# An attention and feed-forward kernel: two PSUM slots become two tensors, nine early masks move to one pair of banks, and the order of work is listed anew

## The chip, the cores and the metric

One Trainium2 chip, one core. The kernel is one launch. The metric is device time in microseconds; the kernel before has a median of 805.13 us over 3 runs (803.35 to 806.81). Lower is better. A program of some 17,900 instructions runs on five engines: TensorE (PE, with its weight loads as PEld), VectorE (DVE), ScalarE (ACT), GpSimd (POOL), and SyncE (SP), which issues DMAs.

## The reference: top-32 attention, then a gated feed-forward layer

```python
# attention: q, k, v are (4, 8, 576, 64)
scores = scale * np.matmul(q, k.transpose(0, 1, 3, 2))
kth = np.partition(scores, -32, axis=-1)[..., -32:-31]
scores = np.where(scores >= kth, scores, -1e9)
attn = softmax(scores);  out = attn @ v
# feed-forward on x, (2304, 512): 4 * 576 tokens, 8 heads * 64
h = x @ w_in                      # w_in is (512, 2048)
g = h * np.tanh(log1p(exp(h)))
return g @ w_out                  # w_out is (2048, 512)
```

All of it is wanted in float32 accuracy. The weights arrive as 64-bit floats.

## The kernel before, in words

**Attention.** The work is cut into 80 units. A unit is one tile of 128 query rows for a pair of heads (for the last 64 rows both heads share one tile). Each head's part of a unit is a slot, a 128 x 576 matrix of scores; there are 144 slots, numbered in order, and several tables (`CB`, `MB`, `PBO`, `PBH`) choose by slot number how a step is done. A unit goes: scores by matmul into the ring psW (line 701), eviction to S by ScalarE (720), eight-at-a-time maxima on VectorE for a threshold guess (736 to 750), a count of what lies below the guess (765 on ScalarE or 769 on VectorE), a multiply that leaves only the values of interest (773), a small rank compare on 9 elements (776), and one more maximum (779) that gives the exact threshold. Then come the mask and the exponential, a reciprocal (850), the division (875 and 877), transposes (900), evictions (906), the product with V (938) and a copy into xr (959 and 979), which holds the tokens for the feed-forward layer.

**The mask** of a slot is done in one of three ways. The usual one takes the exponential of the scores on ScalarE (843) and multiplies it by the comparison with the threshold on VectorE (845). For slots in `MB` ScalarE forms a large penalty (835), GpSimd subtracts it (837) and ScalarE takes the exponential (839). For slots in `PBO` and `PBH` ScalarE forms a relu of threshold minus score in the buffer EM (814; one buffer), TensorE adds score and penalty in PSUM (823, 824), and ScalarE takes the exponential straight from PSUM (827). This third way needs two PSUM banks: those of the output accumulators (psO) for `PBO`, those of the up-projection (psH) for `PBH`. A slot in `PBO` or `PBH` is done by matmul even where `MB` holds it too.

**Feed-forward.** Tokens go in 9 groups of 256. A group's tokens are split in a high and a low part (xh and xl; 1034, 1039 and 1045). The up-projection `m1` (1068) computes hidden blocks of 128 in pairs, 72 pairs in all: each half of a pair is 12 matmuls of 128 x 256 into one half of a slot of 512 columns. A pair is evicted from PSUM to mb by ScalarE (1074) or VectorE (1076), then goes through tanh, arctan and sin on ScalarE (1080, 1099, 1100; in batches, since these need other tables than the exponential), a multiply (1115), a cast to GH (1120 and 1122), a subtraction to GL (1130), and the down-projection (1149 for the first group, 1153 for the others) into psO. Line 1211 or 1213 evicts psO.

**PSUM.** It has eight banks of 512 float32 columns. psW is a ring of four tensors of one bank. The up-projection has two slots, which are two halves of one tensor psHH of 1024 columns; after the last unit two of psW's tensors are lent to it as slots 3 and 4. psO is likewise one tensor psOO of 1024 columns, used as two halves.

**What sets the order.** Each step is an entry of a plan (`P.op`) with an engine, a duration, what it depends on, and what buffer slots it takes and frees. Some entries have several ways, that is, engines that can do them. The list `ORDER` holds, for the main program, the number of each of the 4,931 entries and the way chosen. The plan walks through that list, gives each entry a start time from the durations, sorts by it, and issues the instructions in that sequence; every engine runs its own in order. The waits between engines are then derived from the tensors that the issued instructions read and write. Two things follow the plan's times beside the sequence: filler matmuls on TensorE in long planned gaps, and an extra wait of a GpSimd step for a VectorE step that has just been planned (lines 1285 to 1289).

Of the kernel before, what the change touches and what calls it, by code (L numbers as in the profile page):

```python
# [49 lines left out]
PBO = (2, 8, 12, 16)  # L50
PBH = (0, 2, 6, 10, 20, 28, 31, 138)
# [40 lines left out]
    b"AHT#qu83Xz_T6@Js;k@C!cyX=l%&0k^z%PfFQ%;>Y-A(kI$e~1TNSE#y_}iFxLV8i{Qc9bvR%QEOI6L*&0f*n4(q7o?C{Ff$=yZ$?~EIkn+J#2"
    b"B+PoR@N^>TkXGt?XnApAd~h1eeO73Dkku*N-aPmnni__S7BAOYrMJ_UNYE#dR~anv)HVvF`9}NQ*cV2j(&!A`m3}N=fz|A#I%|0O^!)V=*ZLb9"
    b"EaqQiv?MS{(8PGDuvox)Q<K$x0qa)#2ZgT>4hUXj#@rwtA`vRI!F-d*TG3_eY}RZH3yImhcGJO7$?$bj(iU3+t=7wIJg_-vi>>S-IZFlk*x+4}"
    b"hpms;$16H*4Y6}}h<mer?~dI{%AwnK9>i@_+2^?2C1RInLSk5?>L%AcH#bLlZE)Lvt28M&H6`6WZH33t=-U}F$F}Sa-xGCWYuTaGZ@mvBa8;C_"
    b"tlV~|s<!&nzW47|o*9hY8|SlYM}0(QL)Omyhga3yJAQV1&XK0Xx^s8WHxAwZ5Sf&_yE%G~URvJ83(3PN2M$JEiO)EZy6!=G_T&7A1+7<O4t;Dn"
    b"y7$wu&zByxJ^3<v`D7e7{u!A-yjJ*>ay)MTncTyq&Qm-c^se^qOy+YcJFBQdzxeBTNvwh4k(cp3wCgWM#u$7o0p4%?XM0~63Fe6}TD&B%@B8}x"
    b"bHcZSE=U9?{8)Ov?DU~a1EL~7O)rW~Od03@s+N^BdA)4fBHL{8&Tl#S#6L+^<~CB6Gk>ofp50(=Z!7IAbopwEql2AGh->IIOlq=X{E<qfG=+_B"
    b"VNUx$6yy|@7ABO)6sI3o-gG@&B`NV%otlPMO__(f=H?qK>aj6ZH}960Cs(AXZaHyVD>c1B`}WqfqZ!BVRJ(6mUa1pNbF9|0%6p~m_7j;WPi16g"
    b"-C5-~>|5!xb5~7$-Q%MtA6!57>9c=TR>0}((;sWABUd-no~duByLTq%?wSYtqVDdv(75~F+19nWjrW`Ln$BH#*toZC|DNXT^Iw{tJUpB8=xNKn"  # L100
    b"`<Jg=jLv@?Q*fZY?PBY*k(Q^U2a7Kqh`oC7(37v%#)?Wh#yh)<;|gCKe);X~sr%=iz0PkxpBsDq`H}AvJzX8_mw7iz;uDe*Q*IR8?ELZbS7~=z"
    b"a%x7;rGZ=N$9hX&bzQyL@aApr(aFB!ulrwB^i7|<e(QJH?RW1_l|MK!_59Dwjls$@Ls`|Cq^g>~vvqgwo~wPwg)74jV#wSK3hn*b#`@C@=Re+K"
    b"Qgd?YLwKIN4^6`tK4o7V$^U$<pymFh2VX{;#|XTvX1<4)uROZh^zG|+;yC;2HG#qwK_UJ}KPMjk5S|o?w%J{3^{DV_(dAoL9{>8&I@2aTJ@xm="
    b"(<0H|V(rg5W+f#skNI1Rd9j@(-L?+g(o$WrIJ~?}x0Ah{W7{(xIcEiz=UnPa&tL56aVIQy^>TYs{^Dg+FLCdyeaid$qBUNsC<^p@d-!;+h*3ST"
    b"a+Q{*_QBX5-wrih9X~#jVBf$YLt!%bab6U6B;oMW!Z$DaJKJA%^}Z6J>oNRAlj7GVt`1B|*6%-_X0Uk4x&U!zkpyeKQAzPqq11s8<Ljm-p*Pl)"
    b"n%%No_WI4Ijlt>WCvJvGR+Me1JXv0S>UKs@=FzH}w|$$$2HxEXuibpCuKujlxzk(DSiJuH#`10dyRGkItglC$-<~z};KTduyE$JzZ2KsEV29P`"
    b"!I6fciQ(LPjR#|QHd)6Vmf4ke@lfQ2eA@z9yGxfHoxVQ&bmU9(_{g{Wqw!-&2`!1=l2cNDJ{p(*{(5-uyWEeTkK62jO@5qJQoY7C@heTe^~t2o"
    b"Q-v!(rqbIpj*cq+cD-@SZRXkE<9{eB8q{N@<sDNuJG-W5Pcu$*zp21HfA>P!z3k*|%~RDcx!#_^_Vha7@Z3CVm6<hlRp5Kjn05Ai?I3}c^Io6+"
    b"fLNc`kb7Y$`(ji6LxZo=T4TCei?m5(9W0(zfV;#);QnxL_>m#|K9l(I(`UWQByua|>XmD}g^x$tzBG>(E#@nJ)<S#ol)r<~-swy={@SIjTS6aW"
    b"F?reid^#@Q3<dS{4LrJ^8wI@RSt9hZ_tom9YemJDPY5nrEMPMJeSeJEsvp9hUOz>bEHx4`T_$d9VkTy4F1$>{(xR__#kw`#<`RLylB?GT1<Pz0"  # L110
    b"nEEAYA+>UHT3S}_z;F43e-soCS%<8#@{x+2QHrziQ&Cp^Ya43sV0XkZ-o<~Wq<<a8S1lmaN!=~U)qQiy^|c-wo!1K-7Qb<GLqb@ZM(L*TjOB^9"
# [1232 lines left out]
```

## Time and profile before

| | |
|---|---|
| median of 3 runs | 805.13 us (803.35 to 806.81) |
| profiled execution | 804.39 us, span 802.5 us |
| TensorE busy | 761.6 us (95%), weight loads 597.3 us |
| VectorE, ScalarE, GpSimd busy | 679.3, 658.6 and 518.8 us |
| mean granted TensorE clock | 0.992 of full speed |

The span runs from the first to the last instruction; the execution is 1.9 us longer. Busy time of an engine is the union of its instructions. An engine's idle time is put down to whatever released the instruction after it. Matmuls are pipelined, so one that is shown with 0.28 us is followed by the next after some 0.12.

### The profile page before, as it was taken

What the parts mean: (1) busy time and instruction counts of PE and PEld (TensorE: products, weight loads), DVE (VectorE), ACT (ScalarE), POOL (GpSimd) and SP (SyncE); (2) the same over time, 40 slices, a digit from 0 to 9 for tenths busy, and PEclk for the clock granted to TensorE, in tenths of its full rate; (3) what the DMA queues carried; (4) which work ended last, traced back from release to release, by engine and by line L of the source; (5) the groups of instructions that cost most, each with busy time, mean ns of one, the idle gap of its engine ahead of it and who ended that gap; (6) DMA issues with size and microseconds to landing.
All of it is one profiled execution on the core that took longest, in us unless ns stands there. A gap on an engine that the chain in (4) does not pass through costs nothing.

```text
span 802.5 us, 17921 instructions
## 1 busy us (share of the span) xinstructions
PE 761.6 (95%) x5697; PEld 597.3 (74%) x5697; DVE 679.3 (85%) x3067; ACT 658.6 (82%) x1372; POOL 518.8 (65%) x765
## 2 busy tenths in 40 slices
PE   8789999988999999999999999999999999999995
PEld 5556677755768878768878777787878787889983
DVE  6999999999999889999999998999899989813531
ACT  5999999999899889798999787889898689457540
POOL 3888897888676666778678576765666666313130
PEclk9999999999999999999999999999999999999998
DMA  5424456643324322330222322323242122203343
GB/s 159 149 80 148 127 155 227 234 169 132 129 87 141 90 89 60 101 113 25 84 82 60 127 86 84 93 82 96 67 125 67 59 83 79 83 15 89 89 116 92
DMA packets 56792, 83.70 MB, mean 104 GB/s; under 512 B 5872, under 2 KB 28656, under 8 KB 56688
## 3 DMA queue, kind: packets, MB, share of 16 engines
q1 hardware_dynamic: 56464, 82.19, 33.1%
q8 instruction: 47, 0.77, 0.4%
q14 instruction: 57, 0.47, 0.2%
q10 hardware_dynamic: 224, 0.28, 0.1%
HBM read 66.72 MB, written 8.13 MB: 93 GB/s over the span
## 4 chain that ended last, share of the span: by engine, by line
PE 61%; ACT 14%; DVE 9%; POOL 7%; issue 3%; DMA 3%; SPq 0%; ACTq 0%; POOLq 0%; DVEq 0%
PE psO L1153 19%; PE psH L1068 19%; PE psW L701 7%; PE psW L938 7%; PE psW L900 5%; POOL Y L773 3%; DVE Y L845 2%; ACT S L720 2%; ACT tb L1100 2%; DVE C L736 1%; ACT Y L843 1%; PE psW L1068 1%; DVE M L779 1%; PE psO L1149 1%; ACT WT L906 1%
## 5 line engine op out<-in xcount | busy, mean ns | idle before, releaser
L773 POOL TENSOR_TENSOR Y<-Y,S 128x576 f32<-128x576 f32 x126 | 178.4, 1422 | 27.4 <-DVE Y L845 8.2
L736 DVE MAX8 C<-S 128x8 f32<-128x82 f32 (+1 forms) x1008 | 170.8, 230 | 8.7 <-ACT S L720 7.9
L1068 PE MATMUL psH<-xh,wih 128*128 128x256 f32 x544 | 163.1, 300 | 4.8 <-ACT mb L1074 3.1
L1068 PE MATMUL psH<-xl,wih 128*128 128x256 f32 x544 | 153.6, 282 | 0.0
L1068 PE MATMUL psH<-xh,wil 128*128 128x256 f32 x544 | 153.4, 282 | 0.0
L701 PE MATMUL psW<-KS,QS 64*128 64x288 f32 (+1 forms) x576 | 121.1, 459 | 4.6 <-DMA QS<-in_q_dram 2.1
L720 ACT COPY S<-psW 128x288 f32<-128x288 f32 x288 | 108.9, 406 | 18.5 <-PE psW L701 18.0
L779 DVE MAX8 M<-Y 128x8 f32<-128x585 f32 x144 | 109.0, 760 | 7.8 <-POOL Y L773 5.5
L1068 PEld LDWEIGHTS psH<-xh,wih 128*128 128x128 f32 x544 | 103.7, 191 | 15.5 <-ACT mb L1074 5.8
L1153 PE MATMUL psO<-woh,GH 128*128 128x512 f32 x256 | 107.7, 421 | 0.0
L845 DVE SCALAR_TENSOR_TENSOR Y<-S,M,Y 128x576 f32<-128x576 f32 x120 | 99.4, 841 | 7.2 <-ACT Y L843 6.8
L1068 PEld LDWEIGHTS psH<-xl,wih 128*128 128x128 f32 x544 | 103.7, 191 | 1.5 <-issue 0.2
L1068 PEld LDWEIGHTS psH<-xh,wil 128*128 128x128 f32 x544 | 103.5, 190 | 0.0
L843 ACT ACTIVATE Y<-S,SM 128x576 f32<-128x576 f32 x120 | 93.4, 785 | 11.6 <-DVE M L779 10.9
L1130 POOL TENSOR_TENSOR GL<-mb,GH 128x256 fp32r<-128x256 f32 x93 | 69.4, 750 | 46.2 <-DVE GH L1120 22.5
L900 PE MATMUL psW<-ident,Y 128*128 128x128 f32 (+1 forms) x640 | 82.3, 270 | 10.9 <-ACT Y L877 3.0
L938 PEld LDWEIGHTS psW<-WT,V 128*64 128x64 f32 x1280 | 64.2, 138 | 33.6 <-ACT WX L924 14.8
L900 PEld LDWEIGHTS psW<-ident,Y 128*128 128x128 f32 (+1 forms) x640 | 62.9, 140 | 34.8 <-ACT Y L877 7.2
L938 PE MATMUL psW<-WT,V 128*64 128x128 f32 (+1 forms) x1280 | 81.9, 271 | 6.8 <-ACT WX L924 6.3
L906 ACT COPY WT<-psW 128x512 f32<-128x512 f32 (+1 forms) x142 | 74.5, 553 | 15.5 <-PE psW L900 15.2
L746 DVE MAX8 M<-C 128x8 f32<-128x56 f32 x432 | 83.4, 208 | 1.8
L769 DVE TENSOR_SCALAR_CACHE_REDUCE Y<-S,M 128x576 f32<-128x576 f32 x98 | 78.5, 804 | 7.1 <-PE psW L917 5.5
(167 smaller groups left out, 1720.2 us busy)
## 6 DMA issues: line engine op xcount, KB each, us to landing
WL<-wld SPq DMA_DIRECT2D x104, 256.0 KB, 2.7
V<-in_v_dram SPq DMA_DIRECT2D x28, 320.0 KB, 3.1
mb<-in_moe_w_in_dram SPq DMA_DIRECT2D x16, 512.0 KB, 3.8
mb<-in_moe_w_out_dram SPq DMA_DIRECT2D x16, 512.0 KB, 4.2
KS<-in_k_dram SPq DMA_DIRECT2D x27, 288.0 KB, 3.2
QS<-in_q_dram SPq DMA_DIRECT2D x80, 64.0 KB, 2.7
woh<-mb SPq DMA_DIRECT2D x16, 256.0 KB, 2.9
wld<-woh SPq DMA_DIRECT2D x13, 256.0 KB, 2.5
```

The lines of the kernel that those rows point to most:

```text
L701: nc.tensor.matmul(psW[P.slot[wks[n]]][:, 0:HS], g_("QS", qs)[hp, :], KSt()[hp, rng], start=True, stop=True)
L720: return lambda: eng(St(n)[:, rng], psW[P.slot[w]][:, 0:HS])
L736: nc.vector.max(Ct(n)[:, j, :], St(n)[:, EDGE[j]:EDGE[j + 1]])
L746: cur[n] = P.op("dve", dve(8 * NCH), lambda n=n, r=r: nc.vector.max(M8()[:, n, r, :], Ct(n)), [cur[n]], free=[("C", ck[n])] if r == 2 else ...
L773: y = either(pool2(S), held(S), lambda eng, n=n: eng.tensor_tensor(Yt(n), Yt(n), St(n), op=ALU.mult), [c], prio=pr + 0.5 + OFF[5])
L779: ym.append(P.op("dve", dve(S + PAD), lambda n=n: nc.vector.max(M8()[:, n, 3, :], Yw(n)), [y, x], prio=pr + 0.6 + OFF[6]))
L843: e = P.op("act", acts(S, 1), lambda n=n: nc.scalar.activation(Yt(n), St(n), AF.Exp, scale=scale, bias=SM()[:, 0, n:n + 1]), [nm, ym[n]], ...
L845: mk.append(P.op("dve", held(S, 68), lambda n=n: nc.vector.scalar_tensor_tensor(Yt(n), St(n), th(n), Yt(n), op0=ALU.is_ge, op1=ALU.mult, a ...
L900: nc.tensor.transpose(psW[P.slot[wk]][:, t_ * w:(t_ + 1) * w], Yt(n)[hp, c_:c_ + 128], ident[hp, hp])
L938: nc.tensor.matmul(psX[64 * h:64 * h + 64, 0:n_], lw, rhs, start=t_ == 0, stop=t_ == T)
L1068: nc.tensor.matmul(w, a, b_, start=n == 0, stop=n == len(mm) - 1)
L1153: nc.tensor.matmul(psO[t], c[:, ts_], y, start=f == 0 and n == 0, stop=f == NF - 1 and n == 2)
```

## The change

The two slots of the up-projection become two tensors of 512 columns. The table `PBH` goes. `PBO` becomes (0, 2, 6, 8, 9, 10, 12, 16, 20): slots 0, 6, 10 and 20 move from the up-projection's pair to the accumulators', slot 9 goes from the usual mask to the mask by matmul, slots 28 and 138 go from matmul to the usual mask, and slot 31, which `MB` holds, from matmul to GpSimd's mask. Slots 2, 8, 12 and 16 stay. Some planned durations of small steps change, and `ORDER` is another list.

```diff
-PBO = (2, 8, 12, 16)
-PBH = (0, 2, 6, 10, 20, 28, 31, 138)
+PBO = (0, 2, 6, 8, 9, 10, 12, 16, 20)
...
 ORDER = (
...
     psW = [ps.tile([128, 512], F32, name=f"psW{i}") for i in range(Z["W"])]
-    psHH = ps.tile([128, 1024], F32, name="psH")
     psOO = ps.tile([128, 1024], F32, name="psO")
-    psH = [psHH[:, 0:512], psHH[:, 512:1024]] + psW[0:2]
+    psH = [ps.tile([128, 512], F32, name=f"psH{i}") for i in range(2)] + psW[0:2]
     psO = [psOO[:, 0:512], psOO[:, 512:1024]]
...
-                nm = P.op("pool", 0.15, lambda: nc.gpsimd.tensor_scalar(
+                nm = P.op("pool", 0.19, lambda: nc.gpsimd.tensor_scalar(
...
-                        c = P.op("pool", 0.15, lambda n=n, c24=c24: nc.gpsimd.tensor_scalar(
+                        c = P.op("pool", 0.21, lambda n=n, c24=c24: nc.gpsimd.tensor_scalar(
...
-                    x = either(0.29, 0.129, lambda eng, n=n: eng.tensor_scalar(
+                    x = either(0.38, 0.125, lambda eng, n=n: eng.tensor_scalar(
...
-                lg = P.op("pool", 0.15, lambda: nc.gpsimd.tensor_scalar(
+                lg = P.op("pool", 0.19, lambda: nc.gpsimd.tensor_scalar(
...
-                by = "O" if n0 + n in PBO else "H" if n0 + n in PBH else None
+                by = "O" if n0 + n in PBO else None
...
-                    bk = [(by, key + ("pb", n, i)) for i in range(1 if by == "O" else 2)]
-                    pb = psOO if by == "O" else psHH
+                    bk = [(by, key + ("pb", n, i)) for i in range(1)]
+                    pb = psOO
...
-                    e = P.op("pool", pool2(S), lambda n=n: nc.gpsimd.tensor_tensor(
+                    e = P.op("pool", 1.18, lambda n=n: nc.gpsimd.tensor_tensor(
...
-            rzo = P.op("pool", 0.15, lambda: nc.gpsimd.tensor_scalar(
+            rzo = P.op("pool", 0.24, lambda: nc.gpsimd.tensor_scalar(
...
-            rzo = P.op("dve", 0.13, rz, [rzo, lg], free=[("M8", m8k)], prio=pr + 0.8 + OFF[6])
+            rzo = P.op("dve", 0.07, rz, [rzo, lg], free=[("M8", m8k)], prio=pr + 0.8 + OFF[6])
```

Both lists are compressed, so the diff does not show what they hold. Decoded, each has 4,931 entries. TensorE's part is nearly the same: in both, the first `m1` comes after 24 score steps, 18 transposes and 8 products with V, the 49th after 86, 80 and 40, and the 85th after 60 products with V. The engines chosen for steps with several ways differ as follows (before to after):

| step (line) | GpSimd | VectorE | ScalarE |
|---|---|---|---|
| multiply (773) | 126 to 121 | 18 to 23 | |
| rank compare (776) | 40 to 23 | 104 to 121 | |
| division (875, 877) | 31 to 35 | 5 to 6 | 72 to 67 |
| sum of a row (852, 854) | 38 to 31 | | 42 to 49 |
| high part of tokens (1034, 1045) | 10 to 16 | 5 to 3 | 21 to 17 |
| eviction of a pair (1074, 1076) | | 14 to 10 | 58 to 62 |
| product with the gate (1115) | 49 to 51 | 23 to 21 | |
| cast to GH (1120, 1122) | 22 to 23 | 13 to 6 | 29 to 35 |
| subtraction to GL (1130) | 95 to 90 | 33 to 38 | |

## Rows read from the trace of the kernel before

**Rows 1.** The page, busy time: us, share of the span, instructions.

```profile
PE 761.6 (95%) x5697; PEld 597.3 (74%) x5697; DVE 679.3 (85%) x3067; ACT 658.6 (82%) x1372; POOL 518.8 (65%) x765
```

**Rows 2.** Windows: length, then busy us of each engine with instructions; clock, DMA.

```profile
0.00:200.00 200.00, 178.25 (x1260) 123.39 (x1262) 183.83 (x870) 181.25 (x411) 159.87 (x256) 0.98 0.50 158
200.00:680.00 480.00, 471.90 (x3695) 376.73 (x3693) 446.54 (x2080) 417.94 (x866) 331.31 (x471) 1.00 0.29 88
680.00:802.50 122.50, 111.42 (x752) 97.22 (x748) 48.89 (x119) 59.38 (x97) 27.61 (x39) 0.98 0.28 79
```

**Rows 3.** Groups, whole span: busy us, mean ns, idle us before with releasers.

```profile
L1068 PE MATMUL psH<-xh,wih 128*128 128x256 f32 x544 | 163.1, 300 | 4.8 <-ACT mb L1074 3.1 <-DVE mb L1076 1.5
...
L1068 PEld LDWEIGHTS psH<-xh,wih 128*128 128x128 f32 x544 | 103.7, 191 | 15.5 <-ACT mb L1074 5.8 <-issue 5.0 <-DVE mb L1076 2.2
...
L1074 ACT COPY mb<-psH 128x512 f32<-128x512 f32 x56 | 32.9, 590 | 13.6 <-PE psH L1068 13.5
...
L1076 DVE COPY mb<-psH 128x512 f32<-128x512 f32 x10 | 6.9, 688 | 12.2 <-PE psH L1068 12.0
```

**Rows 4.** Groups of line 1068 from 200 to 680 us.

```profile
L1068 PE MATMUL psH<-xh,wih 128*128 128x256 f32 x372 | 111.8, 301 | 2.1 <-ACT mb L1074 1.6 <-DVE mb L1076 0.3
```

**Rows 5.** Groups of line 1068 from 680 us on.

```profile
L1068 PE MATMUL psH<-xh,wih 128*128 128x256 f32 x96 | 27.7, 289 | 1.6 <-DVE mb L1076 1.1 <-ACT mb L1074 0.5
```

**Rows 6.** Waits from 200 to 680 us: total us, times, longest us.

```profile
ACT mb L1074 <- PE psH L1068: 10.0, 9, 1.5
```

**Rows 7.** Timeline near 700 us: start, us, instruction, idle before.

```profile
699.95 0.28 PE L1068 MATMUL psH<-xh,wil 128*128 128x256 f32 x1
...
701.27 0.28 PE L1068 MATMUL psH<-xl,wih 128*128 128x256 f32 x1
...
701.39 0.28 PE L1068 MATMUL psH<-xh,wil 128*128 128x256 f32 x1
701.70 0.69 DVE L1076 COPY mb<-psH 128x512 f32<-128x512 f32 x1 [2.54 <-PE psH L1068]
...
702.45 0.39 PE L1068 MATMUL psH<-xh,wih 128*128 128x256 f32 x1 [0.78 <-DVE mb L1076]
```

**Rows 8.** Timeline near 645 us.

```profile
645.90 0.28 PE L1068 MATMUL psH<-xh,wil 128*128 128x256 f32 x1
...
646.22 0.59 ACT L1074 COPY mb<-psH 128x512 f32<-128x512 f32 x1 [1.40 <-PE psH L1068]
...
646.85 0.39 PE L1068 MATMUL psH<-xh,wih 128*128 128x256 f32 x1 [0.68 <-ACT mb L1074]
```

**Rows 9.** Timeline near 758 us, where psW is lent to the up-projection.

```profile
757.91 0.68 DVE L1076 COPY S<-psW 128x512 f32<-128x512 f32 x1
...
758.63 0.28 PE L1068 MATMUL psW<-xh,wil 128*128 128x256 f32 x1
```

**Rows 10.** Timeline near 675 us: the mask of slot 138, and what follows.

```profile
674.75 1.02 PE L823 MATMUL psH<-S,ident 128*128 128x512 f32 x2
...
676.09 0.48 PE L1153 MATMUL psO<-woh,GH 128*128 128x512 f32 x1
```

**Rows 11.** Groups, whole span, of the side work that moves.

```profile
L845 DVE SCALAR_TENSOR_TENSOR Y<-S,M,Y 128x576 f32<-128x576 f32 x120 | 99.4, 841 | 7.2 <-ACT Y L843 6.8
...
L776 DVE TENSOR_SCALAR Y<-ranks,SM 128x9 f32<-128x9 f32 x71 | 14.7, 210 | 0.0
...
L773 DVE TENSOR_TENSOR Y<-Y,S 128x576 f32<-128x576 f32 x18 | 14.4, 813 | 0.0
...
L1130 DVE TENSOR_TENSOR GL<-mb,GH 128x256 fp32r<-128x256 f32 x27 | 12.6, 467 | 7.1 <-ACT GH L1122 4.0 <-PE psO L1153 2.8
...
L1120 DVE TENSOR_SCALAR GH<-mb 128x512 fp32r<-128x512 f32 x11 | 4.6, 422 | 11.2 <-PE psO L1153 7.5 <-POOL mb L1115 3.6
```

**Rows 12.** Line 776 on GpSimd: ns min/median/max, starts, forms.

```profile
L776 POOL TENSOR_SCALAR Y<-ranks,SM x27: 329/347/1470, 61.4 to 686.9; 128x9 f32<-128x9 f32 x27
```

More of the change, by code (lines that the diff above doesn't have):

```diff
@@ L92 @@
[L92 to L111, printed above, removed]
@@ new lines @@
+    b"3eweeH5YlmIwia{AyJen!q~QWq0kaB-z2|f(q|aYm2{W}tR36gvH^zTOOy4CB#dQNq{wlW>-z_%n#gn0LITYsO;_&R6*NydZ2qbUb14-Ig$32="
+    b"su`JCyZ4+s8y=~4-tvM~&BeW!6!%AEt6OW-*3~yOuFcI0U7fS0>9Wn00|nQvUeDLEU>RB3z0iz)`D*=!jj=J!2ZsySEx4_{UZ;4|V2fUBiEiA`"
+    b"oe`6p`%2r4^>4hpwfV!?-8c74w|tyuu%W%|wPnZK^7r#AiVW|MT8~d0>gr@4vEp!#K6uD~OrZPlalubQpM}jTt^Pa`6ZtCoQ(Qu_>cmN@Nt-V="
+    b"*5*C7-@Z%B*xK3m_WiPZ{N#tM-0vv|c}E8)cg=v)zS|rXojo?H{ZV-O*S;U4<izLVtm5V};Nhw~t&W{ib@zIP^NH2KyDpyo>q#JLdU<-2$U1&n"
+    b"-b)rza7%sN7HRwIVyHg)dRV^21~fd~&_rwAGE)+PVq`pjleP}g-*4H%MYJVk29>pRIekY6Ga%ATmm9ajfEmCx=NAyx(+>^|U1ca}v2r<QmC*tb"
@@ new lines @@
+    b"V-q1U)8&Cdp+O;mD<s#521SL<4_jd#J}-QMnfPiei%6-6sI}3S!K;H~l2$rO*sM*Kj+U`qBO4*-6ti+&i2SO}DXEIeY3r0!c5bX0#NrdI?Lv2j"
+    b"*@ve)xMXDQ$=ssgye4+_Cii_Fn_YLutExq;SC4c{Tokuqo2PG-##*nf7h)D?@AdZCe_;E%go~GUG~^ugTUfikE_q8{eDu~0#VNT-8T$;EY#SQR"
+    b"Us~_qSn@h`W9-Q0O$ApjUu(Kvc(o|4tTe7=XLIYaH#f?+Y>!VqwChgh;jD@y``eCXAKiNM?e2GbZoN+-Bpm;c(_WcMBz25d9iSzSb=|w$dHX*3"
+    b"<PJ(A^;Ftv`kC&P>3efejDO7AS)IS@0i);aBPOetUGVAP_Cv*KDMshgO^lN=INXPi`TGhdK0h5e+;4hbP(b+0vm<6gN1r_ZHvh%EkouQjzl)el"
+    b"m57P{kPx>xX1U;%wUwl8rgZ75$=_Kr3O{Xr*_S!ml{*yGRvxeT(-1oKw@Gn#<B70o*(xO$r*MyxS9W6dI(vEUTkUpAZVjJz#F@9Q?()?cr!U|d"
@@ new lines @@
+    b"_b99QsxDrbzANi&rrQ2&P3=oMiz3gdN1ZRcn6rEB9-o-Y(RF+G?Qho5s%^TiTc_uj+fctwzwt^=_L8dy4;bWb$jdLN&s$%3)c?lPfXmC4Uv0Xw"
+    b"@#?0cz<0$#E4J4hXl^)oE$RHN`}sw&<=3wl$K9y7{J!K+X-mtsn`N!dCD%6JK73<K+sz}#ZjIeZ{IGR&JotFRor?Hvr62EhoH%xKd+Ytm+wDj1"
+    b"Jvh|<a7Wdrwu#QWCp)^6lTvP-O09m>)p<JkbJw{uY3CoG{nC?ObG-G{!-B&PQp=7!xmP~Kf42MElSjLDKJCls-JN;id(FkHy+2>}^nUICadF_;"
+    b"<NcTR{MwiEJp16_h00g`FMj_y^|UH~YVyF)xl6Cl57g(@4mUh2Xe=pe8hKOK^7l6N^~iKyVR0!IUv?RD^-6O&4R?r8^X4rdlX!$QOn=8d%sP7Q"
+    b"#&z<|V=Wb@IgIzMl-tKY2vlAe9ls+i(k95Qx^wUD{aYtajeYv~d7|yh*YDrNew;kbe@5tj^*zyF9pb-FIG)^b=A!+n_`d2hm+neQOtnw`o&MR0"
@@ new lines @@
+    b">3;A>^3g*+8KL%$vyXeaaJ2&GI-LlvF7DED3cYxu(qm^2**=n+V7I)dY8_V5XHnN;WwICeTkY?wqDAR@vbF!o(}8CRYR{i*CknsVMt!+`$5VAb"
+    b"9o?l#di{?yG!2&1=nN4PrdaYa)4^vw&wB@+VUiv^6lWP4iLwKY=jp!)NJ-n3nz3?c*8Gt4%vCR?IMv+q(q?DPC2A}#EI7AkcPRJ=b4AepeQR<*"
+    b"SVmacS-%<#4vWkV&x^8=tgV-+Yh0bb_Ib`wQ$fSkXxqyNVhUf#zAQa><yx~{@vGO@%Sv9qDOx|eZg7L#(2er9w}%}z#tx5EjBT<{Zh7<e-TSYj"
+    b"ALQc>-8}sHPD<+LG=(iYj~sJy*mZRLxO3%r>)o+Wx6(hhWhhPT&fI%%f7X|rFF(Hh(z^fo<H)=7-(J1{uBiIsQ+risN0*!XiLXChlpi=g{Q14+"
+    b"!bR<FmB~MQPEP%u-lu{6b$UYA%li?XF`0efH(R~uQt#thOy5Di`rL-W*H6^)v7F*Oor1a{pQkuiW=TJOfIuV-H#QYsz1&=S<4Rf4wVT&RTFQ-X"
@@ new lines @@
+    b"YmyI9JdU*LA3j>4M>W1fJBGu*IsW$UyZi4c2D+v}M8ir_)d>Rm)XCE<?k)aylQ!xHM#reY8CEB4+@iYs9*6$vqu{)=o{#h%Fdz1uGtgfk)WzoS"
+    b"eLTh$oDk^yB4qM)zKEgmlYX<`+pR=b3@l4BdirePB2zQVZ=Z#q2m3DeTPb1w;=9;9k@*r9KSaeOEtkBsHWyzYHThH0TE^Dum-H&x-||btSJ?cq"
+    b"wUJYBuu}|?Q3?%n@eh_to=Opx{hQ|KWbZ1jtg<}aIo!>2=W6#g(-9eR-T|uWf#*UZ`2Gg1eX&waW0z*Cmyg!!g}bBnW_pC~Ulg-;O=Q-doalWA"
+    b"vk$B~?|Y#}JErd9Vn3Zr((7`g>Mz$WS-+v-%2I#%Yu6hc!j`=pjC5SLF)u%MlftW^0LA57;#`_qieDELmR=oh9=TBzsI)nLtCMm`#haUDD(g33"
+    b"KC5frdRu<GHTKTCyN46rx7|Oab0pezW8yu&O>Uh>w;k)k;_&UH<8cHXk1CVO2SmM-p5z_NH`5+&VNkT<yHA`_Wl>M-o^kHr&>!)S>RPIO*vcFq"
@@ new lines @@
+    b"(>Lg;?mcVxIM9flp#RmFJ5S)F*^?E0i4#wQH2O6^>1mr-SekyGA3WgxMacZC^|xm~zyB~46cbrsB`j(qu~OXh*K>KJ`3AQ0CVdu4O3QkA|F)B{"
+    b"mvj2INZvupQ6a=-m9w#;@An@+|ClSehW>W9n*8NyrW`gEZeg=<+E>-f!_E57YPD(aDIY$C1<O~Y*)3L4^ix;XP+Fq0bm5vse{m56Oq3=GtA<x6"
+    b"YH5)p{eArwFR@*^jIwgAMsxsGhe`9dUlyYpuugM*V&LKpdfK{l1GbU=#-MGnaekYU7@Jd;ZeOw`-k%j<$VpD!!Q~eWHeEj7SU|{pYsj($;T0l*"
+    b"D}&~(G7DaiwsU7j`YzF3VIiw6tW82KFV%&984-+%5wj7`l(63&zGqEFmZX%eox|S!`!c2LWwII^*H}eHMdZj{-jjXMDdxc1ymaTr=-h&JE=_W="
+    b"`RlK4C|<wO)qSs<N8Gi-O`Dr<6m9X$-hHLSYhP*E_4u0=Er)NFx8Av(vo*o{O`^};wnGs|-W}VveMjZ-dsX}29;knxBy7Lv{)wXvAClWUM8+PR"
@@ L170 @@
+    b"6xrTfZ*Mj)0tQ?iJsrK7kc&Y7V|q~HUrldr07GxM0u7y+s-7OA#RGVQh<^q<tBH2g<2gJA;-FYIWb=cE%RgrlJtXA!1}*jBQ6XZc&X1Tk>hroG"
+    b"DSZH9^Xu#D!@vhR!1LkZfv3-}kD$<x|Nj74kAZU"
 )
```

117 lines of the change are left out of this document (53 added, 64 removed).

## The prediction, made before the changed kernel was run

> **What bounds the kernel now.** I read the engine totals first, then the windows, then the groups of the up-projection, then the timeline at the places which those name. The totals [rows 1] show TensorE busy 95% of the span and VectorE 85%. The windows [rows 2] split this: in the first 200 us TensorE idles 200 - 178.25 = 21.75 us; from 200 to 680 it idles only 480 - 471.90 = 8.1 us while VectorE is busy 446.54 (93%); after 680 nothing but the last groups is left, and VectorE is busy 48.89 of 122.5. So from 200 us on TensorE sets the end, with VectorE close behind until 680. Only what shortens TensorE's work or closes its holes is gained in full, and only after 680 without a doubt.
>
> The holes that the change can touch are those before the up-projection (line 1068). Its first matmuls had 4.8 us of idle time, all put down to the evictions at lines 1074 and 1076; by the weight loads it is 5.8 + 2.2 = 8.0 us. The same evictions waited 13.5 us on ScalarE and 12.0 us on VectorE for line 1068 [rows 3].
>
> The timeline shows what these waits are. At 699.95 a pair of hidden blocks issues its last matmul, which ends at 700.23; its eviction could start there, and VectorE was idle for 2.54 us. It starts at 701.70, just after the last matmul of the next pair's first half (701.39 + 0.28 = 701.67). The next pair's second half then starts at 702.45, just after that eviction (701.70 + 0.69 = 702.39) [rows 7]. Yet the next pair writes the other slot. The same stands at 645: the eviction, for which ScalarE idled 1.40 us, starts at 646.22 after the next half's last matmul (645.90 + 0.28), and the second half starts at 646.85 after the eviction [rows 8]. Neither wait carries data. Eviction and matmul take turns as if the two slots were one buffer, and in the kernel they are two halves of one tensor. Slots borrowed from psW are tensors of their own, and there an eviction runs from 757.91 to 758.59 beside matmuls that go on to 758.63 into the next slot [rows 9]. It is the only overlap among the 72 evictions.
>
> **The change part by part.**
>
> *The two slots as two tensors.* This removes both false waits and adds nothing. The hole is a little longer than the idle figure: 702.45 - 701.39 = 1.06 us from start to start where 0.12 is usual (701.27 to 701.39), so 0.94 lost against 0.78 shown [rows 7]; 0.95 - 0.12 = 0.83 against 0.68 [rows 8]. Both are 1.21 times the figure, so 4.8 stands for 5.8 us. By stretch: 2.1 from 200 to 680 [rows 4], 1.6 after [rows 5], the remaining 1.1 before, or 2.5, 1.95 and 1.35 us. After 680 I count all of it, 1.95, since no other engine is near its limit. From 200 to 680 I count half, 1.25 (ends 0 and 2.5): where TensorE comes earlier, the next late one is a ScalarE or VectorE result. Before 200 TensorE is not the bound; half, 0.65 (ends 0 and 1.35). Sum 3.85 us.
>
> *The evictions earlier.* ScalarE is in order, so what stands behind a held eviction is held too. From 200 to 680 it lost 10.0 us in 9 such waits, 1.5 at most [rows 6]. That stretch has 8.1 - 2.1 = 6.0 us of other TensorE idle time [rows 2, 4], for which earlier ScalarE results can help. The ends are 0 and 6.0; I take a quarter, 1.5 us, because ScalarE is idle 62 us there anyway [rows 2] and most results are not late.
>
> *The masks.* Slot 138 loses its matmul mask: 676.09 - 674.75 = 1.34 us of TensorE in the full stretch [rows 10], counted whole; it gives VectorE one masked multiply of 0.84 us instead [rows 11]. Slot 28 does the same and slot 31 goes to GpSimd's mask, both near 190 us, where TensorE has holes; slot 9 goes the other way. Slots 0, 6, 10 and 20 use the accumulators instead of the up-projection's pair; both are empty until group 0 begins. What can hurt is that all nine now share one pair and one EM buffer, so 8, 9 and 10 queue: the relu of the next stands on ScalarE behind the matmul of the one before, at worst 1.34 us each, twice, in a stretch that TensorE does not set. I put the early masks at 0 (ends 2 us lost, 2 us won, the latter for VectorE's 0.84 us at slot 9 and holes of TensorE near 190 us that two masks fewer may close).
>
> *The order and the engines.* TensorE's order in the new list is nearly the old one. What moves is side work: by the list's choices VectorE gets 17 more rank compares at 0.21 us, 5 more multiplies at 0.81 and 5 more subtractions at 0.47, and with slots 28 and 138 more and slot 9 less one masked multiply at 0.84: 3.6 + 4.1 + 2.3 + 0.8 = 10.8 us [rows 11]. It loses 4 evictions at 0.69 [rows 3] and 7 casts at 0.42 [rows 11], 5.7 us, part of them after 680. GpSimd, which gives most of this work away, is no bound (331 of 480 us busy [rows 2]). Nothing in the trace prices a better or worse interleaving. The nearest rows are the holes of other cause: 6.0 us from 200 to 680 could be closed, and as many could open. I take 0 with ends of 5 us each way.
>
> *Sum.* 3.85 + 1.5 + 1.34 = 6.7 us. The profiled execution took 804.39 us around its span of 802.5, so 797.7; the median of the runs, 805.13, lies 0.74 above that execution, so 798.4 us. The edits to the planner's durations alter no instruction; they matter only through the order.
>
> **Rivals.**
>
> *The gain is absorbed before 680.* If VectorE and ScalarE set the pace of the attention, a TensorE that comes early waits again. Then 1.95 after 680 remains and half of slot 138's mask: 2.6 us, 802.5 us. For it: VectorE's 93%. Against: TensorE's 98% [rows 2].
>
> *More than the holes.* ScalarE's 10.0 us of waits are the head of several chains; if they and the order close the whole 6.0 us of other holes and all 5.8 count, the gain is 5.8 + 6.0 + 1.3 = 13.1 us, 792 us. Against it: most of ScalarE's waits have slack behind them.
>
> *Slower: VectorE becomes the bound from 200 to 680.* The place is the masked part of the attention, the price the added 10.8 us if what is taken from VectorE lies after 680. It decides once VectorE's busy time passes TensorE's: 446.5 + 10.8 = 457 is still under 470. But a VectorE instruction can be longer than its mean while GpSimd works: GpSimd's rank compare has a median of 347 ns and a maximum of 1470 [rows 12], so the two engines do hold each other. With all 10.8 at the end, less 1.95 and 1.34, the time is 805.1 + 7.5 = 812.6; with half of it 807.2. I take 810.
>
> The Trainium skill ("SBUF — State Buffer", section "SBUF: two separate sides") says of this that VectorE, with two SBUF inputs, and GpSimd take a shared port pair as an exclusive lock for a whole instruction. The 1470 ns compare agrees with it; by that rule the ten moved two-input operations stop GpSimd each time, which is a reason to keep the slower case alive.
>
> *The change does not do what it says.* If the turn-taking were the chip's own, two tensors in the same banks would take turns as before; only slot 138 would be left, 803.8 us. The eviction at 757.91 speaks against it [rows 9]. The Trainium skill ("PSUM — Partial Sum Buffer", section "PSUM bank collisions raise a hardware error") says that the chip doesn't stall two engines on one bank but reports an error; by that rule the waits of rows 7 and 8 are the program's, and the trace agrees.
>
> **How the numbers follow.** The forecast has 0.50, the absorbed gain 0.24, the larger gain 0.14, the slower case 0.08, no effect 0.04. A measurement of this kernel tells about 0.5% from no change, that is 4 us: faster means under 801.1, slower over 809.2. The forecast's own spread, 794.5 to 802, comes from the ends of its halves (1.25 and 1.5) and from some of the order's 5 us, and about a tenth of it lies above 801.1. Faster: 0.46 + 0.14 + a little of the absorbed case, 0.62. Slower: most of its case, 0.07. Same: 0.31. For 8 in 10 the range goes from 791, under the larger gain, to 806, over the absorbed case; what is left out is the slower case and the tails.
>
> **What would show it.** Right: evictions out of psH that run beside up-projection matmuls; line 1068's idle time for lines 1074 and 1076 falls from 4.8 to under 1 us; line 1074's wait for line 1068 from 200 to 680 falls from 10.0 to under 4; after 680 the same work takes about 2 us less. Absorbed: those waits gone, but TensorE's idle time from 200 to 680 still near 8 us, now before lines 900, 938 or 701. Slower: VectorE's busy share from 200 to 680 over 96%. The prediction is wrong if the false waits are gone and the time is not under 801, or if early masks queue and the first 200 us grow by more than 3 us.

## The result: 783.9 us, three times the gain that was forecast

The changed kernel takes 783.93 us (median of 4 runs, 782.84 to 784.57) against 805.86 us for the kernel before on the same chip (803.35 to 806.81). The ratio is 0.9731, 95% interval [0.9705, 0.9757]: 21.9 us faster. The forecast was 798.4 us with a range of 791 to 806. Its direction was right, its size was not. The profiled execution took 782.84 us around a span of 781.0.

From line 492 of the kernel before on, the new kernel's lines have a number one lower: the up-projection's matmuls are line 1067, its evictions 1073 and 1075. First come the busy times of the new kernel from its page, which answer to [rows 1].

```profile
PE 754.0 (97%) x5677; PEld 593.7 (76%) x5677; DVE 674.4 (86%) x3087; ACT 657.6 (84%) x1375; POOL 502.0 (64%) x744
```

TensorE was busy 95% and is busy 97%, and VectorE is less busy than before (674.4 us against 679.3), not more. The windows of the new kernel, which answer to [rows 2]:

```profile
0.00:200.00 200.00, 182.67 (x1286) 125.71 (x1287) 188.92 (x905) 187.29 (x430) 158.04 (x256) 0.99 0.51 162
200.00:680.00 480.00, 478.89 (x3790) 386.16 (x3789) 459.13 (x2124) 421.15 (x874) 318.11 (x453) 1.00 0.31 90
680.00:781.00 101.00, 92.44 (x605) 81.85 (x603) 26.40 (x60) 49.16 (x72) 25.81 (x36) 0.98 0.28 80
```

From 200 to 680 us TensorE now idles 480 - 478.89 = 1.1 us, where it idled 8.1 [rows 2]. In the first 200 us it idles 17.3 us, 4.4 less than before, and 26 more matmuls fit in. The groups of the up-projection and its evictions, which answer to [rows 3]:

```profile
L1067 PE MATMUL psH<-xh,wih 128*128 128x256 f32 x544 | 162.2, 298 | 0.0
...
L1067 PEld LDWEIGHTS psH<-xh,wih 128*128 128x128 f32 x544 | 103.4, 190 | 7.4 <-issue 4.1 <-ACT SM L853 0.4 <-ACT S L719 0.4
...
L1073 ACT COPY mb<-psH 128x512 f32<-128x512 f32 x58 | 34.5, 598 | 21.9 <-PE psH L1067 21.9
...
L1075 DVE COPY mb<-psH 128x512 f32<-128x512 f32 x7 | 4.8, 683 | 13.5 <-PE psH L1067 13.5
```

The 4.8 us that the matmuls waited for evictions [rows 3] are gone. The evictions wait longer in sum, 21.9 us on ScalarE, but 19.7 of these lie after 680 us and are waits for data, where TensorE is the last to be ready. From 200 to 680, where [rows 6] had 10.0 us in 9 waits, the waits of the new kernel hold this (total, count, longest):

```profile
ACT mb L1073 <- PE psH L1067: 2.2, 5, 1.0
```

The timeline of the new kernel at 685 us (start, duration, instruction) shows what took the place of [rows 7] and [rows 8]:

```profile
685.29 0.28 PE L1067 MATMUL psH<-xl,wih 128*128 128x256 f32 x1
...
685.65 0.28 PE L1067 MATMUL psH<-xl,wih 128*128 128x256 f32 x1
685.73 0.59 ACT L1073 COPY mb<-psH 128x512 f32<-128x512 f32 x1 [1.72 <-PE psH L1067]
685.77 0.28 PE L1067 MATMUL psH<-xh,wil 128*128 128x256 f32 x1
...
686.25 0.28 PE L1067 MATMUL psH<-xh,wih 128*128 128x256 f32 x1
686.37 0.28 PE L1067 MATMUL psH<-xl,wih 128*128 128x256 f32 x1
```

The eviction of one slot runs from 685.73 to 686.32 while matmuls into the other go on every 0.12 us. Before, one of the 72 evictions overlapped matmuls of the up-projection, out of a borrowed slot [rows 9]; now 27 evictions out of the two own slots do.

### The profile page after: what moved, and what is told of

It is laid out like the page before. It is cut to its first block, busy times and chain, and to the rows that moved or that the text cites. A ratio compares the mean times of both kernels' runs of the same rounds, so it can differ in the third digit from the quotient of the medians.

```text
span 781.0 us, 17888 instructions
## 1 busy us (share of the span) xinstructions
PE 754.0 (97%) x5677; PEld 593.7 (76%) x5677; DVE 674.4 (86%) x3087; ACT 657.6 (84%) x1375; POOL 502.0 (64%) x744
## 4 chain that ended last, share of the span: by engine, by line
PE 70%; DVE 11%; ACT 8%; POOL 6%; issue 2%; DMA 1%; SPq 0%; DVEq 0%; POOLq 0%; ACTq 0%
PE psO L1152 22%; PE psH L1067 20%; PE psW L700 9%; PE psW L937 8%; PE psW L899 6%; DVE C L735 3%; POOL Y L772 3%; PE psO L1148 2%; PE psW L1067 1%; DVE M L778 1%; DVE Y L844 1%; DVE mb L589 1%; DVE mb L585 1%; ACT S L719 1%; DVE C L749 1%
## 5 line engine op out<-in xcount | busy, mean ns | idle before, releaser
L772 POOL TENSOR_TENSOR Y<-Y,S 128x576 f32<-128x576 f32 x121 | 171.1, 1422 | 30.7 <-DVE Y L768 5.7
L700 PE MATMUL psW<-KS,QS 64*128 64x288 f32 (+1 forms) x576 | 123.9, 460 | 3.7 <-DMA QS<-in_q_dram 1.8
L1129 POOL TENSOR_TENSOR GL<-mb,GH 128x256 fp32r<-128x256 f32 x85 | 62.5, 739 | 32.4 <-ACT GH L1121 8.7
```

The lines of the kernel that those rows point to most:

```text
L700: nc.tensor.matmul(psW[P.slot[wks[n]]][:, 0:HS], g_("QS", qs)[hp, :], KSt()[hp, rng], start=True, stop=True)
L772: y = either(pool2(S), held(S), lambda eng, n=n: eng.tensor_tensor(Yt(n), Yt(n), St(n), op=ALU.mult), [c], prio=pr + 0.5 + OFF[5])
```

## Experiments: the parts one by one

Every number is the median of a kernel's runs; the ratio is to the kernel before, run beside it on the same chip, with its 95% interval. NEW and OLD stand for the two lists behind `ORDER`, and edits of `ORDER` are written in these names; OLD's steps are renumbered for the new masks, which shifts three steps of slot 9 slightly. Every run but e7, e8 and e11 has the new masks and the new planned times.

### Tensors and order

**e1: NEW, new masks, one tensor.**

```diff
-    psH = [ps.tile([128, 512], F32, name=f"psH{i}") for i in range(2)] + psW[0:2]
+    psHH = ps.tile([128, 1024], F32, name="psH")
+    psH = [psHH[:, 0:512], psHH[:, 512:1024]] + psW[0:2]
```

> The changed kernel (783.9 us) with its two up-projection slots made halves of one 1024-column PSUM tensor again; list, masks and engines as changed. Theory A (the two tensors are worth what the forecast said, some 6 us, and the new order gives the rest by itself): 789 to 791 us, and the false turn-taking of eviction and matmul is back. Theory B (the new order alone gives nearly everything): 784 to 787. Theory C (the new order is good only where the slots are independent, since it lets evictions lie beside the next pair's matmuls): 795 us or more.

**e2: OLD, new masks, two tensors.**

```diff
-ORDER = NEW
+ORDER = OLD
```

> Two tensors and the new masks, but the old list: each entry of the old list is kept in its place and on its old engine, the entries of slots 9, 28, 31 and 138 put where their old ones stood. Theory A: 798 to 800 us (the forecast's 6 us, no more). Theory B: 802 to 805. Theory C: 796 to 800, and the rest of the 22 us comes only with both.

**e3: OLD, new masks, one tensor** (both edits).

> Old list and old engines as in the run before, new masks, one tensor of two halves: the masks alone. All theories: within 2 us of the kernel before (805.5), about 804, since one 1.34 us mask leaves TensorE. If it is under 801 or over 808 the masks were mis-sized.

Measured: e1 795.70 us, 0.9893 [0.9858, 0.9927]; e2 797.76 us, 0.9925 [0.9897, 0.9952]; e3 811.61 us, 1.0093 [1.0063, 1.0124]; the kernel before, run beside them, 804.18. With the new kernel this is a square:

| | one tensor | two tensors | the tensors' worth |
|---|---|---|---|
| OLD | 811.61 | 797.76 | 13.9 |
| NEW | 795.70 | 783.93 | 11.8 |
| the order's worth | 15.9 | 13.8 | |

The new kernel's 783.93 us has its own runs of the kernel before beside it (805.86); by the ratios the two differences with it are 13.0 and 15.6 us instead of 11.8 and 13.8, so a difference is known to some 2 to 3 us. Within that the two parts add up: neither needs the other, and each is worth 12 to 16 us. None of the theories as stated holds. That of the tensors had the mechanism and half the size; that of the order alone is refuted by e1. Theory C named the right ranges for e1 (795 or more) and e2 (796 to 800), but its reason is refuted by e3: the order is worth as much with one tensor as with two. e3 is a miss of its own: the rest of the change, masks and planned times, costs 7.4 us in the old list. So part of what the order is worth in this square only gives that back; against the kernel before, e1 with list, masks and planned times together is 8.5 us faster (804.18 to 795.70).

The groups of e1 and its evictions, in the new order with the false waits back (its lines have the numbers of before):

```profile
L1068 PE MATMUL psH<-xh,wih 128*128 128x256 f32 x544 | 162.8, 299 | 6.4 <-ACT mb L1074 5.9 <-DVE mb L1076 0.4
...
L1068 PEld LDWEIGHTS psH<-xh,wih 128*128 128x128 f32 x544 | 103.3, 190 | 16.8 <-ACT mb L1074 9.6 <-issue 3.4 <-DVE mb L1076 1.1
...
L1074 ACT COPY mb<-psH 128x512 f32<-128x512 f32 x58 | 34.5, 597 | 37.1 <-PE psH L1068 37.1
```

The idle time of 6.4 us is not the whole loss. A matmul is shown with 0.28 us though the next starts after 0.12, so a stop of up to 0.16 us hides behind the end of the one before. The distance from start to start has no such cover. Summed over the 144 first matmuls of a half, worked out from the traces, and over all of TensorE's instructions by kind (us):

```
                                before     e3     e2     e1   after     e5     e6
before the 144 halves             25.9   25.0   18.9   26.0    17.1   17.8   19.0
within and before transposes      92.9   95.5   91.3   92.1    89.9   92.7   89.9
within and before scores (701)   100.0  102.4   99.5  101.4   100.2  102.6  100.1
before the products with V        33.6   35.5   35.6   28.3    28.2   28.9   28.8
```

From e1 to the new kernel the halves come 8.9 us closer; of what is left of 12.8 us in the spans (793.8 to 781.0) most lies at the transposes and scores, 3.4 us.

e1 and the new kernel give TensorE the same 5,677 matmuls in the same order, so the lead of the new kernel can be taken at each of them, and where it grows is where the two tensors pay. The same holds for e3 and e2 with their 5,679. Worked out from the traces, the lead in us when the slower of the two stands at:

```
                     200 us   680 us   720 us   the end
e1 to after             0.2      9.3     13.0      12.8
e3 to e2                4.3     11.3     14.7      15.3
```

In the new order 9.1 us come between 200 and 680 us, 3.7 in the next 40, and nothing after that.

**e5 and e6: which of the two false waits.** Both are the new kernel with one wait put back by hand, for the two own slots alone. In e5 an eviction also waits for the last half issued into the other slot; in e6 a half also waits for the last eviction issued.

```diff
...
             o.fn()
+            kind, hk = P.kind.get(o.seq, (None, None))
+            if kind and P.slot[hk] < 2:
+                if kind == "copy" and "half" in last:
+                    tc.add_manual_dep(made[0], last["half"], mybir.DependencyInfo(
+                        mybir.DependencyClass.Sync, mybir.DependencyReason.SCHED_ONLY), reason="turn")
+                last[kind] = made[-1].name
```

> The new kernel (783.9 us) with two tensors, and one of the two false waits put back by hand: an eviction out of either slot of the up-projection also waits for the last half that has been issued into the other slot. TensorE waits for nothing new. The one tensor with both false waits took 795.7, so 11.8 us are to be explained. Theory 'TensorE stands': the cost is TensorE standing before a second half, which needs the other wait too; then this kernel is at 784 to 786.5. Theory 'evictions late': the cost comes by way of the late eviction (ScalarE and VectorE behind it, in order), whoever waits; then it is at 789 to 794.

> The new kernel (783.9 us) with two tensors, and the other false wait put back by hand: a half of the up-projection also waits for the last eviction issued out of either slot. Evictions may start at once, beside the next half. Theory 'TensorE stands': this is the wait on which TensorE stands; if it costs by itself, 788 to 793. Theory 'only both together': an eviction (0.65 to 0.75 us) that starts when its pair is done is over before the next half (12 matmuls at 0.12 us, 1.4 us) is, so this wait has already been met: 784 to 786, and the 11.8 us of one tensor come only when the eviction is late and TensorE then waits for it. Theory 'evictions late': also 784 to 786.

Measured: e5 789.84 us, 0.9815 [0.9793, 0.9837]; e6 785.61 us, 0.9764 [0.9741, 0.9786]. Late evictions alone cost 5.9 us, the halves' wait alone 1.7, which the intervals do not tell from nothing (the spans give 6.3 and 2.7); both together cost 11.8. Some 4 us come only when an eviction is late and TensorE then waits for it. For e5 the theory 'evictions late' holds and 'TensorE stands' does not; for e6 the range of the other two theories, 784 to 786, holds. The same groups of e5, then of e6 (the eviction on ScalarE is line 1075 in both):

```profile
L1068 PE MATMUL psH<-xh,wih 128*128 128x256 f32 x544 | 162.3, 298 | 0.7 <-ACT mb L1075 0.7
...
L1075 ACT COPY mb<-psH 128x512 f32<-128x512 f32 x58 | 34.5, 597 | 34.2 <-PE psH L1068 34.2
```

```profile
L1068 PE MATMUL psH<-xh,wih 128*128 128x256 f32 x544 | 162.3, 298 | 0.8 <-ACT mb L1075 0.8
...
L1075 ACT COPY mb<-psH 128x512 f32<-128x512 f32 x58 | 34.6, 598 | 21.9 <-PE psH L1068 21.9
```

In e5 the up-projection hardly stops (17.8 us before its halves against 17.1), yet 5.9 us are lost. They stand in the table at the transposes (+2.8) and the scores (+2.4). ScalarE works in order, so the likely way is that what it had behind a held eviction reached TensorE late; the releasers only point that way (before the transposes the matmuls waited 2.1 us for ScalarE's eviction of scores instead of 1.5, and 1.6 for GpSimd's division instead of nothing), and no run isolates it. The first rival, that only TensorE's own standing costs, is refuted for half of the sum.

### Where in the order

**e4: NEW's sequence, OLD's engines.** Each step at its new place, by the engine that OLD chose for it.

```diff
-ORDER = NEW
+ORDER = [(step, OLD_way[step]) for step, way in NEW]
```

> The changed kernel with the new sequence, but each entry that has several ways on the engine that the old list chose (311 entries differ). If the gain comes from the sequence: 784 to 788 us. If it comes from the other choice of engines (GpSimd relieved): 794 us or more. A mixed order can also be worse than both, since the sequence was made for its engines; over 800 would say that, and not be proof for either.

Measured: 858.63 us, 1.0674 (856.78 to 859.33). It tells the two apart no further: the sequence was made for its engines, and with others it is worse than either list.

**e9 and e10: spliced at the 22nd unit.** e9 is below; e10 has NEW and OLD exchanged.

```diff
-ORDER = NEW
+ORDER = NEW[:k] + [x for x in OLD if x not in NEW[:k]]
```

> Two tensors and new masks; the new order up to the last matmul of the 22nd attention unit (about 200 us), and from there what is left in the old order. All old took 797.8, all new 783.9. At the 20th unit the all-new kernel is 9.3 us ahead of the all-old one (180.1 against 189.4), at the 24th 9.7, at the end 13.9. Theory 'early': two thirds of the order's gain lie in the first 200 us and stay when the rest is old, 787 to 789.5. Theory 'spread': a lead over the old order is given back where the work is bound by other engines, 792 to 796. Theory 'one piece': the old rest doesn't fit the new start, 797 or more.

> The reverse: the old order up to the last matmul of the 22nd attention unit, then what is left in the new order; two tensors, new masks. Theory 'early': 792 to 795 (the last third, 4.5 us, of 797.8). Theory 'spread': 788 to 791. Theory 'one piece': 797 or more.

Measured: e9 788.05 us, 0.9790 [0.9769, 0.9810]; e10 796.48 us, 0.9904 [0.9884, 0.9924]. NEW up to some 200 us brings 797.76 - 788.05 = 9.7 us of the 13.8, and they stay. The rest of NEW brings 4.1 us more behind its own start, but behind OLD's start only 1.3, which its interval does not tell from e2's. The theory "early" holds for e9; for e10 its range, 792 to 795, was missed, since the rest of NEW is worth less behind OLD's start.

Windows of the first 200 us show where, first of e2 (OLD), then of the new kernel; both have two tensors and the same masks. Third come two windows of the kernel before, with its old masks.

```profile
0.00:30.00 30.00, 24.93 (x135) 16.79 (x135) 23.55 (x143) 22.50 (x49) 16.87 (x35) 1.00 0.54 169
30.00:60.00 30.00, 22.38 (x162) 14.51 (x161) 26.31 (x122) 26.78 (x66) 24.28 (x39) 1.00 0.30 91
...
140.00:200.00 60.00, 50.53 (x348) 34.58 (x348) 54.31 (x247) 52.42 (x122) 50.84 (x74) 0.91 0.50 164
```

```profile
0.00:30.00 30.00, 25.41 (x142) 17.07 (x142) 24.71 (x145) 23.12 (x53) 18.25 (x37) 1.00 0.54 172
30.00:60.00 30.00, 27.43 (x187) 17.35 (x187) 28.48 (x142) 28.34 (x68) 27.10 (x45) 1.00 0.41 126
...
140.00:200.00 60.00, 55.41 (x374) 35.37 (x373) 57.27 (x272) 57.21 (x132) 48.70 (x71) 0.97 0.54 171
```

```profile
30.00:60.00 30.00, 24.28 (x158) 15.34 (x159) 28.02 (x132) 27.26 (x66) 25.70 (x41) 0.94 0.31 90
...
140.00:200.00 60.00, 54.21 (x376) 35.85 (x376) 56.63 (x257) 55.98 (x129) 52.16 (x74) 0.97 0.53 179
```

TensorE does 187 matmuls instead of 162 between 30 and 60 us, and 374 instead of 348 between 140 and 200; VectorE and ScalarE are also busier there. Only the first of the two is a gain over the kernel before, which does 158 matmuls from 30 to 60 us; from 140 to 200 it does 376, so there NEW gives back what the new masks cost OLD (e11, below, does 342). By the end of the 22nd unit's products the new kernel is at 204.2 us, e1 at 204.4, the kernel before at 211.5 and e2 at 214.1: of the 9.9 us between NEW and OLD, 7.3 are a lead over the kernel before and 2.6 are OLD's delay with the new masks and times.

### The masks and the planned times

**e7: the kernel before with the planned times of the new one; e8: before, with slots 0, 6, 10 and 20 in the accumulators' pair; e11: before, with the four masks of another kind** (slot 9 by matmul, 28 and 138 by VectorE, 31 by GpSimd).

```diff
-                nm = P.op("pool", 0.15, lambda: nc.gpsimd.tensor_scalar(
+                nm = P.op("pool", 0.19, lambda: nc.gpsimd.tensor_scalar(
...
-                    e = P.op("pool", pool2(S), lambda n=n: nc.gpsimd.tensor_tensor(
+                    e = P.op("pool", 1.18, lambda n=n: nc.gpsimd.tensor_tensor(
```

```diff
-PBO = (2, 8, 12, 16)
-PBH = (0, 2, 6, 10, 20, 28, 31, 138)
+PBO = (0, 2, 6, 8, 10, 12, 16, 20)
+PBH = (28, 31, 138)
```

```diff
-PBO = (2, 8, 12, 16)
-PBH = (0, 2, 6, 10, 20, 28, 31, 138)
+PBO = (2, 8, 9, 12, 16)
+PBH = (0, 6, 10, 20)
```

> The kernel before (one tensor, its order, its masks) with the eight planned times of the new kernel. Its instructions and their order on each engine stay; what the plan's times still decide is which buffer each operation gets, how many filler matmuls TensorE does, and where GpSimd is made to wait for VectorE. The old order with the new masks and these times, one tensor, took 811.6 us, 7.4 over before (804.2). Theory 'masks': this kernel is at 803 to 806. Theory 'plan's times': it is at 809 to 813.

> The kernel before (one tensor, its order, its planned times) in which the masks of slots 0, 6, 10 and 20 use the accumulators' pair as in the new kernel; slots 9, 28, 31 and 138 stay as they were. The same 7.4 us are in question. Theory 'one pair, one queue': the early masks wait for each other and for that pair, 807 to 811. Theory 'plan's times' or 'the four other masks': 803 to 806.

> The kernel before (one tensor, its order and planned times) with the four masks alone that change their kind: slot 9 by matmul, slots 28 and 138 by VectorE's multiply, slot 31 by GpSimd; slots 0, 6, 10 and 20 stay in the up-projection's pair. All of the change but order and tensors cost 7.4 us; its planned times alone 1.9 to 2.7, the move of the four others nothing. Theory 'sum': these four cost the rest, 808 to 811 (GpSimd and VectorE do near 190 us what TensorE did, and the old order has no room for it). Rival 'only together': each part alone costs little and the old list fails only with all of them, 803 to 806.

Measured: e7 806.68 us, 1.0023 [1.0005, 1.0042]; e8 804.01 us, 0.9990 [0.9974, 1.0005]; e11 809.64 us, 1.0055 [1.0038, 1.0072]. The planned times cost some 2 us, the pair in common nothing, the four masks 4.4: 6.3 of e3's 7.4. e8 refutes the queue at one pair, which I had put first, and meets the range of its rivals; e7 missed both of its ranges by little; e11 met that of the sum. The timeline of e11 at slot 31 (its lines are four lower than before) shows the price:

```profile
161.12 0.77 DVE L775 MAX8 M<-Y 128x8 f32<-128x585 f32 x1 [0.76 <-POOL Y L769]
...
161.91 2.51 POOL L1005 TENSOR_TENSOR woh<-woh,WL 128x512 fp32r<-128x512 f32 x2
164.39 0.84 POOL L758 TENSOR_SCALAR blog<-M 128x1 f32<-128x1 f32 x2
165.30 0.19 POOL L748 TENSOR_SCALAR SM<-M 128x2 f32<-128x2 f32 x1
165.57 0.19 POOL L828 TENSOR_SCALAR SM<-M 128x1 f32<-128x1 f32 x1
165.79 0.78 ACT L831 ACTIVATE Y<-S,SM 128x576 f32<-128x576 f32 x1 [2.69 <-POOL SM L828]
...
167.63 1.12 PE L934 MATMUL psW<-WT,V 128*64 128x64 f32 x16 [3.78 <-ACT WX L920]
```

The threshold of slot 31 is ready at 161.89. GpSimd's mask begins with a small multiply of 0.19 us (828), and in OLD's queue that stands behind two subtractions of weights and three small steps, until 165.57. ScalarE's relu waits 2.69 us for it, ScalarE's next copy comes late, and TensorE waits 3.78 us. The same stands in e2 at 167.43. This hole is most of the price: behind the kernel before, e11 is 0.8 us late at the end of the 16th unit's products (158.3 against 157.5), 4.6 at the 18th's (179.1 against 174.5) and 3.7 at the end of the spans (806.2 against 802.5). NEW was made with these masks.

### The same remedy at the end

**e12: in the last group the second accumulator is a borrowed slot** in place of the other half of psO, for its matmuls (below) and its evictions.

```diff
     psO = [psOO[:, 0:512], psOO[:, 512:1024]]
+    psLast = [psO[0], psW[2]]
...
-                            nc.tensor.matmul(psO[t], c[:, ts_], y,
+                            nc.tensor.matmul((psLast if g == NG - 1 else psO)[t], c[:, ts_], y,
```

> The new kernel (783.9 us), with the same remedy at the end: in the last group the second accumulator is a borrowed slot, a tensor of its own, instead of the other half of psO. In the trace of the new kernel TensorE stands 0.46 us at 771.93 until the eviction of the first accumulator (771.50 + 0.37) is over, though it goes on into the second; and the last evictions come one after the other (773.00, 773.46, 773.86). Theory 'turn-taking, here too': evictions of the first accumulator run beside the last matmuls, the 0.46 goes and the chain of the last three copies gets one shorter, 0.8 to 1.3 us in all, 782.6 to 783.1: less than the timing resolves, so the trace decides. Rival: the stand moves elsewhere, 783.9, and the copies still come one by one.

Measured: 781.84 us (781.64 to 783.14), 0.9732 [0.9711, 0.9753], the ratio of the new kernel; span 780.0 against 781.0. The timing does not tell them apart. The ends of the two timelines do, first the new kernel's, then e12's:

```profile
771.50 0.37 ACT L1210 COPY V<-psO 128x256 f32<-128x256 f32 x1 [4.44 <-PE psO L1152]
771.93 0.51 PE L1152 MATMUL psO<-wol,GH 128*128 128x512 f32 x1 [0.46 <-ACT V L1210]
...
773.00 0.42 DVE L1212 COPY V<-psO 128x256 f32<-128x256 f32 x1 [4.47 <-PE psO L1152]
773.46 0.37 ACT L1210 COPY KS<-psO 128x256 f32<-128x256 f32 x1 [1.58 <-DVE V L1212]
773.86 0.42 DVE L1212 COPY KS<-psO 128x256 f32<-128x256 f32 x1 [0.44 <-ACT KS L1210]
```

```profile
771.10 0.37 ACT L1211 COPY V<-psO 128x256 f32<-128x256 f32 x1 [3.74 <-PE psO L1153]
771.14 0.39 PE L1153 MATMUL psW<-WL,GH 128*128 128x512 f32 x1
...
771.51 0.42 DVE L1213 COPY V<-psO 128x256 f32<-128x256 f32 x1 [2.69 <-ACT V L1211]
...
772.50 0.37 ACT L1211 COPY KS<-psW 128x256 f32<-128x256 f32 x1 [1.03 <-PE psW L1153]
772.91 0.42 DVE L1213 COPY KS<-psW 128x256 f32<-128x256 f32 x1 [0.97 <-ACT KS L1211]
```

Both copies of the first accumulator now lie beside matmuls, and the last copy ends at 773.33 instead of 774.28, 0.95 us earlier, within what was expected (0.8 to 1.3).

## Why the prediction was right in kind and wrong in size

**What bounds the kernel: right for the stretch from 200 us on, and not used.** TensorE sets the end there. Closing its holes was worth the full amount (478.89 us busy of 480), where I counted half. By the leads from e1 to the new kernel the two tensors brought 0.2 us before 200 us, 9.1 from 200 to 680 and 3.5 after, where I had 0.65, 1.25 + 1.5 and 1.95. The signs that I had named for being right all came, but they show the mechanism and not its size.

**The two slots: the mechanism was right, the term was mis-sized.** Evictions and matmuls did take turns without need, and two tensors end it. The terms 3.85 + 1.5 = 5.35 us measured 11.8 in the new order and 13.9 in the old. Two steps failed. The 5.8 us, which I took as TensorE's own loss and then cut by half, came from idle time with a factor from two long holes; the short ones that hide behind a matmul's shown end were left out. From start to start 8.9 us went at the halves in the new order (e1 to after), 6.1 in the old (e3 to e2). And a quarter of 6.0 for ScalarE's part was too little: late evictions alone cost 5.9 us (e5), the end of the range that I gave them.

**The masks.** Nothing for the early ones was right for the four that moved (e8) and wrong for those of another kind: with slot 138 I expected a gain of 1.34 us, and in the old order the four together lost 4.4 (e11). Slot 31's mask on GpSimd put a 0.19 us step in the wrong place of that engine's queue. In the new order no run separates them. The planned times were no part of the sum, because I held that they alter no instruction; e7 has four matmuls more than the kernel before (5,701 against 5,697) and is some 2 us slower.

**The order: the step that failed most, together with the masks.** I put it at 0 with 5 us each way, from the 6.0 us of other holes between 200 and 680; against OLD with the new masks it was worth 13.8 us. List, masks and planned times together, which the sum had at 1.34, brought 8.5 (e1 against before), and 7.1 of these stand by the end of the 22nd unit (204.4 us against 211.5). The room was in the same rows: TensorE idled 21.75 us in the first 200 us [rows 2], and a list searched anew could close it. I read that stretch as one that TensorE does not bound and left it out of the sum, though what it saves moves all that follows. I also read the lists by net counts (17 more compares on VectorE), while 311 of the 4,931 steps change their engine (e4); VectorE's busy time fell by 4.9 us where I had worked out a rise.

**The ledger**, in the order in which the runs give it: other masks and times +7.4, two tensors -13.9, order -13.8, sum -20.3 (804.2 to 783.9). In the other order: list, masks and times -8.5 (e1), two tensors -11.8. The sum had -1.34 and -5.35.

**The rivals.** "More than the holes" was nearest, 792 us, and still 8 short. The absorbed gain and the slower VectorE did not come; rank compares and multiplies moved, but VectorE did not become the bound (459.13 of 480 us busy from 200 to 680). That the two engines hold each other is borne out on GpSimd's side: in the kernel before, the 1470 ns compare of [rows 12] starts at 243.65 and ends at 245.12, and two VectorE multiplies with two inputs run one after the other from 243.57 to 244.99. On VectorE's side no price shows: its multiplies take 794 ns on average in the new kernel and 813 before. "Does not do what it says" is refuted by the overlaps.

**What stays open:** which of the new list's early moves count most, since e4 could not part sequence from engines; what the four masks cost in the new order; and what the two tensors alone bring to the kernel before, since no run has them with its own masks and list.

## What to carry to other kernels

Two buffers that are halves of one tensor can be made to take turns with each other; look in the timeline for an eviction that starts only when the other buffer's matmuls end, and give each buffer a tensor of its own. Price such a wait by the distance from start to start and by what stands behind the held instruction, not by the idle column alone. When an order is searched anew, its room is all the idle time of the engine that sets the end, the start of the kernel included, and a list is no neutral part of a change: it fits the steps that it was made for, so its worth is measured with those.
